# More bfloat16 filler products on TensorE: ahead of the state's update, of chunk 1's transposes, and of the rows of chunks 3, 4 and 5

## The chip, the cores and the metric

The kernel runs on one core of a Trainium2 chip. The time is device time in microseconds (us) of one execution; lower is better. The engines are named as in the profile: PE is TensorE's matrix multiplication and PEld its loading of weights, DVE is VectorE, ACT is ScalarE, POOL is GpSimd, and SP is the engine that issues the transfers between memories (SPq its queue).

## The reference

A recurrent attention layer (four sequences, eight heads, 768 steps, 40 values a head) is followed by a feed-forward layer with a leaky ReLU whose slope `alpha` differs by channel. The kernel computes the recurrence in chunks of 128 steps.

```python
for t in range(S):
    m_new = np.maximum(f[t] + m, i[t])
    f_stab = np.exp(f[t] + m - m_new); i_stab = np.exp(i[t] - m_new); m = m_new
    C = f_stab * C + i_stab * outer(v[t], k[t]);  n = f_stab * n + i_stab * k[t]
    y[t] = sigmoid(o[t]) * (C @ q[t]) / np.maximum(np.abs(n @ q[t]), 1.0)
x = y as (B * S, H * D)            # 3072 x 320
h = x @ w_in                       # 320 x 2048
g = np.maximum(h, 0) + alpha * np.minimum(h, 0)
out = g @ w_out                    # 2048 x 320
```

## The kernel before

**Tiles.** The 24 chunks (n = 0 to 23, six for each sequence) have 128 tokens and eight heads each. Two chunks make a group of 256 tokens for the feed-forward layer, twelve groups in all. For a chunk, `stage_a` brings q and k into channel order (transposes into `pq` and `pk`), `update` makes the state's increment (`pu`, from the keys `kd` weighed by their decay), and `stage_b` makes the decays `E` of the even and the odd heads (`E{n}_0`, `E{n}_1`: exponentials on ACT, the triangle cut out on POOL), the scores `pS`, their product with the decays (DVE, into `E`), the part from the state (`from_state`: `pI`, times `eT` into `T`) and the rows of the chunk (`values`: `pH`, scores times values). `T` plus `pH` gives `hv`; `gated` divides (`r`), multiplies the sigmoid of the output gate by it (`og`) and writes the rows `xn`; `x_by_channel` transposes them into `p1` and `p2`, and `split_x` cuts them into two float32r parts.

**Feed-forward.** `up` makes `ph` (2 x 256 tokens by 128 hidden channels, sixteen products), a scaled ReLU on ACT (`g`) and two DVE instructions for the leaky slope; `gh` (ACT) and `gl` (DVE for the first two groups) are its two parts. `down` adds 24 products to `po`. `fp` counts pairs of 128 hidden channels, 0 to 7. The weights are loaded as 64-bit numbers, joined on DVE from their two halves (`t_wi`, `t_wo`, `t_wr`: an ACT pass, a shift, an or) and cut into two parts (`WH`, `WL`, `OH`, `OL`, `W2`). Groups 0 and 1 run interleaved while the weights still come in.

**The gate's tile.** `og` has one buffer for a whole sequence. `load_gate(b + 1)` fills it by six transfers on SP after the last chunk of sequence b has been gated, and `open_gate` makes the sigmoid over it on ACT in one instruction, ahead of which ACT loads the table of that function.

**Buffers for products.** Attention takes its PSUM tiles from `psa`, which takes two tags in turn, with two buffers each. While group 1 of the feed-forward layer uses the buffers of tag "b", all of `psa` has the two of tag "a":

```python
turns[:] = ["a", "a"]
self.po = [ps_a.tile([P, 512], F32, tag="b", name=f"po{g}_{j}")[:, :DM] for j in range(GC)]
```

**Order.** The first group (chunks 0 and 1) is written out by hand: the words of `ORDER` name the steps, and each engine is held to that order. `warm12` in it means twelve bfloat16 products of the identity matrix (taken as 128 x 256 numbers) into a tile that nobody reads (L942). Behind that group a scheduler puts the instructions of each engine in order from its own estimate of their times, so a change at one place moves instructions far behind it; each engine then runs its instructions strictly in that order.

Of the kernel before, what the change touches and what calls it, by code (L numbers as in the profile page):

```python
# [11 lines left out]
BF16 = mybir.dt.bfloat16  # L12
# [5 lines left out]
def kernel(ctx: ExitStack, tc: tile.TileContext, q, k, v, i_gate, f_gate, o_gate, w_in, w_out, alpha, out):  # L18
    nc = tc.nc
    B, H, S, D = q.shape  # L20
    DM, DFF = w_in.shape
    P = 128
# [66 lines left out]
    def load_qk(n):  # L89
        b, c = divmod(n, NC)  # L90
        t0 = c * P
        for j, src in enumerate((q, k)):
            nc.sync.dma_start(by_token_of(n, j), src[b, :, t0 : t0 + P, :].rearrange("h p d -> p h d"))
# [30 lines left out]
    def open_gate(b, c0=0, c1=NC):  # L124
        og = o_tiles[b][:, c0:c1]
        nc.scalar.activation(og, og, AF.Sigmoid)


    def by_parity(x, par):

        return x.rearrange("p (r two) e -> p two r e", two=2)[:, par]

    kds = {}

# [14 lines left out]
    def update_steps(n):  # L149
# [22 lines left out]
        for par in range(2):  # L172
            r = slice(64 * par, 64 * par + D)
            to = by_parity(new[r], par)
            if c == 0:
                nc.vector.tensor_copy(to, by_parity(pu3[r], par))
            else:
                if n not in CP:
                    gam = gamB[r, b * H + par : (b + 1) * H : 2, c : c + 1].broadcast_to([D, NPR, VA])
                    nc.vector.tensor_tensor(to, by_parity(old[r], par), gam, ALU.mult)  # L180
                nc.vector.tensor_tensor(to, to, by_parity(pu3[r], par), ALU.add)
# [113 lines left out]
    def values(n, E, busy=lambda: None):  # L295

        pH = psa(f"pH{n}")
        va = va_t[n // GC % NV][:, n % GC]
        for i in range(H):
            if i % 2 == 0:  # L300
                busy()
            par, p = divmod(i, NPR)
            h = 2 * p + par
            nc.tensor.matmul(
                pH[:, h * VA : (h + 1) * VA], E[par][:, p * P : (p + 1) * P], va[:, h], start=True, stop=True
            )
        return pH[:, : H * VA].rearrange("p (h e) -> p h e", e=VA)
# [93 lines left out]
    def stage_b(n):  # L401
# [45 lines left out]
        if c > 0:  # L447
            *_, T = from_state(n, qf, Q)
        hv = values(n, Es) if n < NBF else values_by_parts(n, Es)
        if c > 0:  # L450
            nc.vector.tensor_tensor(T, T, hv, ALU.add)
# [61 lines left out]
    def attention(n0):  # L513
# [42 lines left out]
    SGP = range(6, 24)  # L556
    OBA = range(0)
    V0, V1 = 0, 2
    ORDER = """dq0 dq1 dw0 dw2 warm24 dv0 dw1 dw4 do1 dw3 do2 scan lf0a lf0b li0 lf0z L0 bj0 qT0 qc0 kT0 kc0 warm12 sp00
        bTt bTc l3a l3b alT l3c l3d warm6 wt0 ex00 sc00 l3e ms00 warm3 sp01 ewj ex01 ms01 sc01 warm3 eeL wg00 wTt eTt  # L560
        wTc eTc lf1a lf1b warm3 w0s wg01 sp10 alC ex10 ms10 warm3 sp11 ex11 qT1 w1s kT1 kc1 w0j0 warm4 li1 wd0 w0j1 w2s
        u0m qc1 u0c v0 w0h w0l w1j0 L1 w2j0 warm2 sc10 w1j1 warm2 w2j1 wd1 wg10 fsm fst sc11 ms11 warm6 dv1 dq3 wg11 og1
        lpa lpb bj1 dq2 dL dx2 w1h g0r dx0 g0g lpc lpd lpe g0x g0p w1l dx1 v1 x0 warm4 tadd g1r g1g s0a w2h g1x g1p w2l x1
        s1a s1d warm3 s0d og2"""

    class FeedForward:
# [196 lines left out]
    def fetch_in(i):  # L763
        if i < DFF // 512:
            pending["in", i] = [load_w_in(i, kt) for kt in range(2)] + ([] if i % 2 else [load_w_rest(i)])

    def fetch_out(fp):
        if fp < NP:
            if fp >= 2 and 2 * fp % NB == 0:
                out_block(2 * fp // NB)  # L770
            pending["out", fp] = [load_w_out(2 * fp)]
# [31 lines left out]
    def first_group():  # L803
# [125 lines left out]
        def x_first(n):  # L929
            if n == 0:  # L930
                p1.append(psa("p1_0"))
                p2.append(psa("p2_0"))
            x_by_channel(0, n, p1[0], p2[0])

        junk = ps_o.tile([P, DM], F32, tag="o0", name="warm")

        dense = ident.bitcast(mybir.dt.bfloat16)

        def warm(n=1):

            for _ in range(n):
                nc.tensor.matmul(junk[:, : 2 * P], dense[:, :P], dense, start=True, stop=True)  # L942


        t0, u0 = slice(0, GT), slice(1, GT + 1)
# [67 lines left out]
        def later_decays():  # L1013
# [26 lines left out]
            bj1=lambda: nc.gpsimd.tensor_tensor(bj[:, t1], li[:, t1], L[:, t1], ALU.subtract),  # L1040
            wt0=lambda: weights(0, GC, nc.gpsimd),
            ewj=lambda: nc.scalar.activation(wj[:, :GT], wj[:, :GT], AF.Exp),
            eeL=lambda: nc.scalar.activation(eL[:, P:GT], L[:, P:GT], AF.Exp),
            wd0=lambda: weighed(0), wd1=lambda: weighed(1),
            v0=lambda: got.update(h0=values(0, [E[0, 0], E[0, 1]], lambda: warm(V0))),
            v1=lambda: got.update(h1=values(1, [E[1, 0], E[1, 1]], lambda: warm(V1))),
            og1=lambda: open_gate(0, 0, GC), og2=lambda: open_gate(0, GC, NC),
            tadd=lambda: nc.vector.tensor_tensor(got["T"], got["T"], got["h1"], ALU.add),
            x0=lambda: x_first(0), x1=lambda: x_first(1),
# [7 lines left out]
            dq2=lambda: load_qk(2), dq3=lambda: load_qk(3), dL=lambda: nc.sync.dma_start(L_d, L),  # L1057
            dx0=lambda: fetch_out(0), dx1=lambda: fetch_out(1), dx2=lambda: fetch_in(2),
# [21 lines left out]
        for j in range(3):  # L1080
# [123 lines left out]
```

## Time and profile before

| | |
|---|---|
| median of 3 runs | 499.66 us (497.86 to 503.6) |
| the profiled execution | 500.96 us, of which 499.2 us from the first to the last instruction |
| mean granted TensorE clock | 0.990 |
| PE busy | 477.7 us (96%) |
| DVE, ACT, POOL busy | 321.6, 321.6, 304.8 us |

The busy share of PE is an average over very different stretches; what a change costs or brings is read from the stretch in which it lies. A row of the timeline has the start, the duration, the engine, the line, the operation with its operands, and in brackets how long the engine had stood idle and what ended that.

### The profile page before, as it was taken

What the parts mean: (1) busy time and instruction counts of PE and PEld (TensorE: products, weight loads), DVE (VectorE), ACT (ScalarE), POOL (GpSimd) and SP (SyncE); (2) the same over time, 40 slices, a digit from 0 to 9 for tenths busy, and PEclk for the clock granted to TensorE, in tenths of its full rate; (3) what the DMA queues carried; (4) which work ended last, traced back from release to release, by engine and by line L of the source; (5) the groups of instructions that cost most, each with busy time, mean ns of one, the idle gap of its engine ahead of it and who ended that gap; (6) DMA issues with size and microseconds to landing.
All of it is one profiled execution on the core that took longest, in us unless ns stands there. A gap on an engine that the chain in (4) does not pass through costs nothing.

```text
span 499.2 us, 11801 instructions
## 1 busy us (share of the span) xinstructions
PE 477.7 (96%) x4463; PEld 457.2 (92%) x4463; DVE 321.6 (64%) x676; ACT 321.6 (64%) x700; POOL 304.8 (61%) x393
## 2 busy tenths in 40 slices
PE   8889889989999999999899999999999999999997
PEld 7778879989989999989799999989999999999997
DVE  6889999934577686764395686567586575642321
ACT  3869697656587677756976677677886673343332
POOL 6632262306469889839498789858878755243242
PEclk9989997999999999999999999999999999999999
DMA  9999976345676566597557575769663130000000
GB/s 169 228 189 278 229 203 183 82 79 125 145 181 146 92 166 156 102 166 158 116 143 135 129 141 121 162 166 156 117 175 83 32 97 1 1 27 1 28 1 26
DMA packets 173922, 61.60 MB, mean 123 GB/s; under 512 B 140154, under 2 KB 166122, under 8 KB 173866
## 3 DMA queue, kind: packets, MB, share of 16 engines
q1 hardware_dynamic: 173786, 60.75, 55.3%
q8 instruction: 35, 0.57, 0.5%
q14 instruction: 21, 0.17, 0.1%
q10 hardware_dynamic: 80, 0.11, 0.1%
HBM read 36.90 MB, written 4.03 MB: 82 GB/s over the span
## 4 chain that ended last, share of the span: by engine, by line
PE 62%; DVE 8%; DMA 8%; ACT 8%; SPq 6%; issue 3%; POOL 3%; ACTq 0%; DVEq 0%; POOLq 0%
PE po L615 25%; PE ph L585 4%; PE ph L588 3%; PE ph L586 3%; PE ph L589 3%; PE ph L591 3%; PE ph L587 3%; PE ph L592 3%; PE ph L590 3%; DMA wo<-in_moe_w_out_dram 3%; PE pH L340 3%; PE pS L434 2%; SPq L678 2%; ACT E L418 2%; SPq L122 2%
## 5 line engine op out<-in xcount | busy, mean ns | idle before, releaser
L607 POOL TENSOR_TENSOR gl<-g,gh 128x512 fp32r<-128x512 f32 x80 | 102.9, 1287 | 62.2 <-ACT gh L606 55.0
L598 DVE SCALAR_TENSOR_TENSOR g<-g,oma,ph 128x256 f32<-128x256 f32 x160 | 69.8, 476 | 76.9 <-ACT g L594 73.1
L615 PE MATMUL po<-OH,gh 128*128 128x320 f32 x368 | 111.3, 314 | 0.0
L615 PE MATMUL po<-OL,gh 128*128 128x320 f32 x368 | 109.6, 311 | 0.0
L594 ACT ACTIVATE g<-ph 128x512 f32<-128x512 f32 x96 | 57.2, 596 | 43.7 <-PE ph L592 31.8
L615 PE MATMUL po<-OH,gl 128*128 128x320 f32 x368 | 71.9, 316 | 1.3 <-POOL gl L607 1.3
L606 ACT CAST gh<-g 128x512 fp32r<-128x512 f32 x80 | 49.5, 619 | 33.3 <-DVE g L598 32.0
L615 PEld LDWEIGHTS po<-OH,gh 128*128 128x128 f32 x368 | 69.0, 188 | 0.4 <-ACT gh L606 0.2
L615 PEld LDWEIGHTS po<-OL,gh 128*128 128x128 f32 x368 | 69.2, 188 | 0.2 <-DVE OL L714 0.2
L585 PE MATMUL ph<-XH,WH 128*128 128x256 f32 x192 | 58.5, 305 | 1.3 <-DVE g L598 0.9
L615 PEld LDWEIGHTS po<-OH,gl 128*128 128x128 f32 x368 | 56.9, 188 | 1.8 <-POOL gl L607 1.8
L418 ACT ACTIVATE E<-Lb,bT 128x128 f32<-128x128 f32 x160 | 50.9, 393 | 7.5 <-PE pH L340 7.2
L589 PE MATMUL ph<-X,W 128*128 128x256 f32 x192 | 55.2, 288 | 0.0
L586 PE MATMUL ph<-XH,WH 128*128 128x256 f32 x192 | 54.9, 286 | 0.0
L588 PE MATMUL ph<-XH,WL 128*128 128x256 f32 x192 | 54.6, 284 | 0.0
L591 PE MATMUL ph<-XL,WH 128*128 128x256 f32 x192 | 54.6, 284 | 0.0
L592 PE MATMUL ph<-X2L,W 128*128 128x256 f32 x192 | 54.5, 285 | 0.0
L587 PE MATMUL ph<-XH,WL 128*128 128x256 f32 x192 | 54.4, 284 | 0.0
L590 PE MATMUL ph<-XL,WH 128*128 128x256 f32 x192 | 54.2, 282 | 0.0
L422 POOL TENSOR_SCALAR_AFFINE_SELECT E<-E 128x512 f32<-128x512 f32 x44 | 30.0, 683 | 36.4 <-ACT E L418 36.4
L327 ACT CAST E<-pS 128x512 bf16<-128x512 f32 x72 | 41.8, 585 | 13.9 <-DVE pS L325 9.1
L585 PEld LDWEIGHTS ph<-XH,WH 128*128 128x128 f32 x192 | 36.6, 191 | 2.3 <-issue 1.1
(198 smaller groups left out, 1146.0 us busy)
## 6 DMA issues: line engine op xcount, KB each, us to landing
Lb<-L_d SPq DMA_DIRECT2D x20, 512.0 KB
wo<-in_moe_w_out_dram SPq DMA_DIRECT2D x8, 640.0 KB
wi<-in_moe_w_in_dram SPq DMA_DIRECT2D x8, 512.0 KB
qn<-in_q_dram SPq DMA_DIRECT2D x24, 160.0 KB
kn<-in_k_dram SPq DMA_DIRECT2D x24, 160.0 KB
va<-in_v_dram SPq DMA_DIRECT2D x24, 160.0 KB
og<-in_o_gate_dram SPq DMA_DIRECT2D x24, 160.0 KB
out_dram<-ob SPq DMA_DIRECT2D x11, 320.0 KB
```

The source lines that it names most:

```text
L418: nc.scalar.activation(E[:, p * P : (p + 1) * P], Lb[:, h] if Lb is not None else pb[:, p * P : (p + 1) * P], AF.Exp, bias=bT[:, c, b * H ...
L585: nc.tensor.matmul(dst, WH[half][:, 0, hs], XH[:, 0], start=True, stop=False)
L586: nc.tensor.matmul(dst, WH[half][:, 1, hs], XH[:, 1], start=False, stop=False)
L587: nc.tensor.matmul(dst, WL[half][:, 0, hs], XH[:, 0], start=False, stop=False)
L588: nc.tensor.matmul(dst, WL[half][:, 1, hs], XH[:, 1], start=False, stop=False)
L589: nc.tensor.matmul(dst, W2[:, fs], X2, start=False, stop=False)
L590: nc.tensor.matmul(dst, WH[half][:, 0, hs], XL[:, 0], start=False, stop=False)
L591: nc.tensor.matmul(dst, WH[half][:, 1, hs], XL[:, 1], start=False, stop=False)
L592: nc.tensor.matmul(dst, W2[:, fs], X2L, start=False, stop=True)
L598: nc.vector.scalar_tensor_tensor(out=y[:, e], in0=gt[:, e], scalar=oma[:, f : f + 1], in1=ph[:, e], op0=ALU.mult, op1=ALU.add)
L607: (nc.vector if g < 2 else nc.gpsimd).tensor_tensor(gl, y, gh.bitcast(F32), ALU.subtract)
L615: nc.tensor.matmul(po[j], x[:, e, j * P : (j + 1) * P], W[f // NB][:, f % NB], **ends)
```

## The change

Twelve more filler products stand in the first group ahead of `u0m` (the products of chunk 0's state update) and twelve ahead of `x1` (the transposes of chunk 1's rows). `values`, which makes the rows of chunks 2 to 5, gets filler products too: four in chunk 3, fourteen in chunk 4 and four in chunk 5, written into the very tile `pH` that the chunk's own products then overwrite.

```diff
+    def dense(dst, k):
+        x = ident.bitcast(BF16)
+        for _ in range(k):
+            nc.tensor.matmul(dst[:, : 2 * P], x[:, :P], x, start=True, stop=True)
...
     def values(n, E, busy=lambda: None):
         pH = psa(f"pH{n}")
+        dense(pH, FILL.get(n, 0))
...
+    FILL = {3: 4, 4: 14, 5: 4}
...
-        u0m qc1 u0c v0 w0h w0l w1j0 L1 w2j0 warm2 sc10 ...
+        warm12 u0m qc1 u0c v0 w0h w0l w1j0 L1 w2j0 warm2 sc10 ...
-        ... s0a w2h g1x g1p w2l x1
+        ... s0a w2h g1x g1p w2l warm12 x1
...
         def warm(n=1):
-            for _ in range(n):
-                nc.tensor.matmul(junk[:, : 2 * P], dense[:, :P], dense, start=True, stop=True)
+            dense(junk, n)
```

Behind the first group the scheduler's order changes too, on every engine, up to the middle of the first two feed-forward groups (about a fifth of the run); behind that the order is the same. Lines of the changed kernel are seven or eight higher than before (L304 is L311, for one). Three places matter for what follows.

The first is PE at the rows of chunk 4 (`pH4`). Before, the scores of the odd heads are followed at once by the rows, and these by the transposes of chunk 3's rows (`p1_1`):

```order
L438 MATMUL pS4_1_891<-qf4_709,kf0_129 128x128 x4
L304 MATMUL pH4_1002<-va0_79,E4_0_803 128x42 x4
L304 MATMUL pH4_1002<-va0_79,E4_1_885 128x42 x4
L462 MATMUL p1_1_815<-ident_72,xn1_695 128x128 x2
L358 MATMUL pI4_995<-C0_85,qf4_709 128x84 x4
```

In the changed kernel the transposes stand first, then fourteen pairs of a load and a filler product (one pair is shown), then the rows:

```order
L445 MATMUL pS4_1_919<-qf4_733,kf0_129 128x128 x4
L469 MATMUL p1_1_843<-ident_72,xn1_719 128x128 x2
L137 LDWEIGHTS ident_72
L137 MATMUL pH4_1030<-ident_72 128x256
...
L311 MATMUL pH4_1030<-va0_79,E4_0_831 128x42 x3
L469 MATMUL p2_1_844<-ident_72,xn1_719 128x128
L311 MATMUL pH4_1030<-va0_79,E4_0_831 128x42
L311 MATMUL pH4_1030<-va0_79,E4_1_913 128x42 x3
L365 MATMUL pI4_1023<-C0_85,qf4_733 128x84 x4
```

What moved: the transposes went ahead of the rows, and the fillers stand between both.

The second is DVE around the gating of chunk 5 (`r5`, then `og0`, which is the gate's tile of sequence 0). Before:

```order
L598 SCALAR_TENSOR_TENSOR ph0_5_1112<-g0_5_1129,oma_74,ph0_5_1112 128x256
L607 TENSOR_TENSOR gg1_0_1107<-ph1_0_1086,gg1_0_1107 128x512
L598 SCALAR_TENSOR_TENSOR ph0_5_1112<-g0_5_1129,oma_74,ph0_5_1112 128x256
L451 TENSOR_TENSOR T5_1465<-T5_1465,pH5_1467 128x336
L196 COPY C0_85<-pu6_1594 40x4x42 x2
L714 TENSOR_TENSOR OL3_1144<-t_wo14_1391,OH3_1143 128x640
L385 SCALAR_TENSOR_TENSOR r5_1477<-T5_1465 128x8
L389 RECIPROCAL r5_1477<-r5_1477 128x8
L607 TENSOR_TENSOR gl0_5_1134<-ph0_5_1112,gh0_5_1133 128x512
L392 TENSOR_TENSOR og0_181<-og0_181,r5_1477 128x320
```

And in the changed kernel:

```order
L615 TENSOR_TENSOR gg1_0_1149<-ph1_0_1128,gg1_0_1149 128x512
L458 TENSOR_TENSOR T5_1507<-T5_1507,pH5_1509 128x336
L722 TENSOR_TENSOR OL3_1186<-t_wo12_1367,OH3_1185 128x640
L392 SCALAR_TENSOR_TENSOR r5_1523<-T5_1507 128x8
L396 RECIPROCAL r5_1523<-r5_1523 128x8
L399 TENSOR_TENSOR og0_181<-og0_181,r5_1523 128x320
L722 TENSOR_TENSOR OL3_1186<-t_wo14_1433,OH3_1185 128x640
L606 SCALAR_TENSOR_TENSOR ph0_5_1154<-g0_5_1171,oma_74,ph0_5_1154 128x256 x2
L615 TENSOR_TENSOR gl0_5_1176<-ph0_5_1154,gh0_5_1175 128x512
L202 COPY C0_85<-pu6_1640 40x4x42 x2
```

What moved: six instructions that stood ahead of `og0` (the second `OL3`, both of `ph0_5`, `gl0_5` and the two copies of the state) now stand behind it.

The third is ACT where the gate of sequence 1 is opened (`og1`). Before, the ReLU of group 1's third pair (`g1_2`) stands ahead of it:

```order
L606 CAST gh0_6_1240<-ph0_6_1219 128x512
L594 ACTIVATE g1_2_1281<-ph1_2_1264 128x512
L126 ACT_TABLE_LOAD
L126 ACTIVATE og1_1483<-og1_1483 128x1920
L606 CAST gg1_2_1285<-ph1_2_1264 128x512
```

And in the changed kernel:

```order
L614 CAST gh0_6_1282<-ph0_6_1261 128x512
L126 ACT_TABLE_LOAD
L126 ACTIVATE og1_1529<-og1_1529 128x1920
L602 ACTIVATE g1_2_1323<-ph1_2_1306 128x512
L614 CAST gg1_2_1327<-ph1_2_1306 128x512
```

What moved: the ReLU `g1_2` went behind the table load and the sigmoid.

More of the change, by code (lines that the diff above doesn't have):

```diff
@@ L561 @@
         wTc eTc lf1a lf1b warm3 w0s wg01 sp10 alC ex10 ms10 warm3 sp11 ex11 qT1 w1s kT1 kc1 w0j0 warm4 li1 wd0 w0j1 w2s
-        u0m qc1 u0c v0 w0h w0l w1j0 L1 w2j0 warm2 sc10 w1j1 warm2 w2j1 wd1 wg10 fsm fst sc11 ms11 warm6 dv1 dq3 wg11 og1
-        lpa lpb bj1 dq2 dL dx2 w1h g0r dx0 g0g lpc lpd lpe g0x g0p w1l dx1 v1 x0 warm4 tadd g1r g1g s0a w2h g1x g1p w2l x1
+        warm12 u0m qc1 u0c v0 w0h w0l w1j0 L1 w2j0 warm2 sc10 w1j1 warm2 w2j1 wd1 wg10 fsm fst sc11 ms11 warm6 dv1 dq3 wg11 og1
+        lpa lpb bj1 dq2 dL dx2 w1h g0r dx0 g0g lpc lpd lpe g0x g0p w1l dx1 v1 x0 warm4 tadd g1r g1g s0a w2h g1x g1p w2l warm12 x1
         s1a s1d warm3 s0d og2"""
@@ L935, in first_group @@
         junk = ps_o.tile([P, DM], F32, tag="o0", name="warm")
-        dense = ident.bitcast(mybir.dt.bfloat16)
         def warm(n=1):
-            for _ in range(n):
-                nc.tensor.matmul(junk[:, : 2 * P], dense[:, :P], dense, start=True, stop=True)
+            dense(junk, n)
         t0, u0 = slice(0, GT), slice(1, GT + 1)
```

## The prediction

> **What bounds the kernel now.** The page gives PE 96% of the span, which is an average. The table by stage says more. Its columns are the stretch and its length in us, then the busy time of PE, PEld, DVE, ACT and POOL with their instructions in brackets, the granted TensorE clock, the share of the DMA engines, and GB/s.
>
> ```profile
> 27.00:57.00 30.00, 27.24 (x245) 24.56 (x245) 26.82 (x62) 21.07 (x42) 6.27 (x9) 0.94 0.99 234
> 57.00:72.00 15.00, 12.33 (x107) 10.68 (x106) 14.02 (x26) 14.92 (x39) 7.32 (x9) 1.00 0.81 205
> 72.00:98.10 26.10, 24.83 (x186) 24.55 (x187) 25.75 (x48) 19.32 (x42) 9.36 (x11) 0.87 0.54 148
> 98.10:109.90 11.80, 10.21 (x79) 9.95 (x78) 4.24 (x9) 5.96 (x8) 1.04 (x2) 1.00 0.54 100
> 109.90:499.20 389.30, 379.27 (x3648) 366.80 (x3648) 230.65 (x495) 244.72 (x537) 262.99 (x327) 1.00 0.49 106
> ```
>
> From 109.9 us on, PE is busy for 379.27 of 389.30 us at full clock, and its order there does not change. So the change is worth what it does to the moment at which that stage starts. Before it, the transfers are full to 57 us (share 0.99), ACT (14.92 of 15.00) and DVE bind to 72, DVE binds to 98.1 (25.75 of 26.10), and then nobody is full: PE waits. The chain of waits and the timelines of POOL, SP, ACT and PE show for what:
>
> ```profile
> 98.19 0.81 POOL L394 TENSOR_TENSOR xn<-T,og 128x320 f32<-128x320 f32 x1 [1.46 <-DVE og L392]
> 99.03 4.46 SPq L122 DMA_DIRECT2D og<-in_o_gate_dram  x6
> 106.30 1.28 ACT L126 ACT_TABLE_LOAD   x1 [1.53 <-DMA og<-in_o_gate_dram]
> 109.31 0.57 ACT L606 CAST gg<-ph 128x512 fp32r<-128x512 f32 x1
> 109.92 0.41 PE L615 MATMUL po<-OH,gg 128*128 128x320 f32 x1 [1.61 <-ACT gg L606]
> ```
>
> Chunk 5's rows (98.19) free the gate's only tile, its six transfers start at 99.03 and are in at 106.30, table load and sigmoid hold ACT to 109.31, and only then comes the cast for which PE idles 1.61 us. This chain starts the last stage.
>
> **The clock.** Windows cut where the granted clock changes:
>
> ```profile
> 15.55:18.96 3.41, 1.80 (x17) 1.48 (x15) 3.41 (x3) 3.40 (x11) 3.33 (x5) 1.00 0.88 192
> 18.96:22.37 3.41, 3.29 (x42) 3.26 (x43) 3.17 (x7) 3.33 (x6) 1.64 (x2) 1.00 0.93 222
> 29.20:32.61 3.41, 1.96 (x15) 1.20 (x14) 2.90 (x8) 1.94 (x5) 1.76 (x2) 1.00 1.22 274
> 32.61:36.02 3.41, 3.41 (x18) 3.41 (x17) 2.60 (x8) 3.37 (x5) 0.00 (x0) 0.50 0.33 120
> 70.16:73.57 3.41, 1.91 (x15) 1.73 (x15) 3.41 (x6) 3.33 (x8) 2.07 (x3) 1.00 0.78 149
> 73.57:76.98 3.41, 3.41 (x18) 3.41 (x18) 3.32 (x5) 3.41 (x10) 2.34 (x3) 0.50 1.06 351
> 76.98:80.39 3.41, 3.41 (x18) 3.41 (x18) 3.41 (x9) 3.29 (x8) 0.73 (x1) 0.50 0.92 237
> ```
>
> Three stretches of 3.41 us run at 0.50, which costs PE 3 x 3.41 x 0.5 = 5.1 us of work; two of them follow a stretch in which PE was busy for under 2 us. That is the most that fillers can win by the clock. The Trainium skill (TensorE: Matmul & The Clock Gate, Part 1) gives a free-running window of about 3.4 us, with which the 3.41 us here agree, and drops the clock only after an idle window, advising against gaps over some 3 us; by that, gaps under 2 us would cost nothing and these fillers would be pure extra work. The trace disagrees with the second half: 1.91 busy us of 3.41 were followed by 0.50. Yet 1.80 (15.55) was followed by full clock, so busy time alone does not settle it.
>
> **Part by part.** PE around the fillers of the first group, with the pace of a filler, and the product that waits in chunk 4 with what it waits for:
>
> ```profile
> 19.08 0.51 PE L161 MATMUL pu<-va,kd 128*40 128x42 f32 x16 [1.74 <-ACT kf L270]
> 24.46 1.04 PE L942 MATMUL warm<-ident 128*128 128x256 bf16 x8
> 25.37 0.64 PE L304 MATMUL pH<-va,E 128*128 128x42 f32 x4
> 30.62 0.41 PE L462 MATMUL p<-ident,xn 128*128 128x128 f32 x2 [1.14 <-DVE xn L394]
> 72.08 0.68 DVE L440 TENSOR_TENSOR E<-pS,E 128x512 f32<-128x512 f32 x1
> 72.81 2.98 PE L304 MATMUL pH<-va,E 128*128 128x42 f32 x16 [1.48 <-DVE E L440]
> ```
>
> A filler takes (25.37 - 24.46) / 8 = 0.114 us. **Ahead of the update**, twelve take 1.37 us, inside the 1.74 for which PE stood idle there: nothing (1.37 if that wait were gone). **Ahead of chunk 1's transposes**, 1.37 us stand against an idle time of 1.14: 0.2 us late, and the throttled stretch at 32.61 should go, 1.7 us of PE work. What is late next is not PE:
>
> ```profile
> 40.46 0.58 ACT L269 COPY kf<-pk 64x512 f32<-64x512 f32 x1 [0.98 <-PE pk L218]
> 56.48 0.79 ACT L688 ACTIVATE t_wo<-wo 128x640 f32<-128x640 f32 x1 [1.21 <-DMA wo<-in_moe_w_out_dram]
> ```
>
> ACT waited 0.98 us for PE at 40.46, the bound of this gain, and at 56.48 it waits 1.21 us for weights that come in when they come in: I take 0, between a gain of 0.98 and a loss of 0.2.
>
> **Chunk 4's fourteen**, 1.60 us, are meant for the 1.48 us of idle at 72.81. But `pH` started at the end of the DVE product at 72.08, the second half of the decays, although its first products read the first half: what it waited for is the buffer, which the odd heads' scores still held (with "a" alone, two buffers, the second tile ahead). The filler writes the same tile, so it inherits that wait and stands behind the idle time, not in it. PE then does 1.60 of filler, 1.88 of `pH` (the same 16 products at full clock, 91.20 below), and the rest: if the fillers at least spare the stretches at 73.57 and 76.98, PE gets back 3.41 and pays 1.60, which is 1.8 early at 80.5; if one stretch remains, it is where it was. What PE needs next comes from DVE, which is full there: at 87.45 it starts the products of `gh`, cast at 85.93 behind a long row of DVE work. So 0, between 1.8 gained and 1.6 lost. **Chunk 3's four**, 0.46 us, lie where PE idles 15.00 - 12.33 = 2.67 us: 0, at worst 0.46. **Chunk 5's four** wait for their buffer likewise and put 0.46 us on PE's path ahead of `pH`.
>
> **The order** moves more. DVE and PE as they were around the gating of chunk 5:
>
> ```profile
> 87.45 0.40 PE L615 MATMUL po<-OH,gh 128*128 128x320 f32 x1
> 91.20 1.88 PE L304 MATMUL pH<-va,E 128*128 128x42 f32 x16
> 97.20 0.31 PE L615 MATMUL po<-OH,gh 128*128 128x320 f32 x1
> 85.93 0.58 ACT L606 CAST gh<-ph 128x512 fp32r<-128x512 f32 x1 [0.72 <-DVE ph L598]
> 93.01 0.48 DVE L598 SCALAR_TENSOR_TENSOR ph<-g,oma,ph 128x256 f32<-128x256 f32 x1
> 93.41 0.68 DVE L607 TENSOR_TENSOR gg<-ph,gg 128x512 fp32r<-128x512 f32 x1
> 94.00 0.47 DVE L598 SCALAR_TENSOR_TENSOR ph<-g,oma,ph 128x256 f32<-128x256 f32 x1
> 94.81 0.66 DVE L196 COPY C<-pu 40x168 f32<-40x168 f32 x2
> 95.39 0.81 DVE L714 TENSOR_TENSOR OL<-t_wo,OH 128x640 fp32r<-128x640 f32 x1
> 96.12 0.62 DVE L385 SCALAR_TENSOR_TENSOR r<-T 128x8 f32<-128x8 f32 x1
> 97.02 0.69 DVE L607 TENSOR_TENSOR gl<-ph,gh 128x512 fp32r<-128x512 f32 x1
> 97.62 0.48 DVE L392 TENSOR_TENSOR og<-og,r 128x320 f32<-128x320 f32 x1
> ```
>
> Six instructions go behind `og`. By start to next start: the two `ph` 0.40 each (93.01 to 93.41), the copies 0.58, `OL` 0.73, `gl` 0.60, together **2.71 us**. DVE is full, so `og` comes 2.71 earlier, at 94.9, if its inputs keep up: `T` needs `pH`, which goes ahead of `ph0_5` on PE and so comes some 2 us earlier there. POOL's rows, the transfers and the sigmoid follow: sigmoid done at 109.31 - 2.71 = 106.60.
>
> Against this, the ReLU of the third pair now stands behind the sigmoid. Its length with what follows is read one pair earlier:
>
> ```profile
> 100.53 0.60 ACT L594 ACTIVATE g<-ph 128x512 f32<-128x512 f32 x1 [0.88 <-PE ph L592]
> 102.21 0.58 ACT L606 CAST gh<-ph 128x512 fp32r<-128x512 f32 x1 [1.08 <-DVE ph L598]
> ```
>
> From ReLU to the end of the cast: 102.79 - 100.53 = 2.26 us, where the cast alone took 0.57 (109.31): **1.65 us** are added (both ends of that price: 1.65 as read, 0 if the chain is not what PE waits for). PE goes on at 106.60 + 2.26 + 0.04 = 108.9 instead of 109.92.
>
> Would PE be there by then? Without its wait it arrived at 109.92 - 1.61 = 108.3. It has 0.46 of fillers more, and `ph0_5`, whose halves now wait behind `og`, gives its cast at 98.10 (the end of `og`) - 2.71 + 0.73 + 0.80 + 0.58 = 97.5, where PE took it at 97.20 before. So 108.3 to 108.8, just ahead of the chain: the fillers are hidden by 0.1 to 0.6 us, and if the chain came sooner they would cost up to 0.46.
>
> **Sum:** -2.71 + 1.65 = -1.06 us. The profiled execution took 500.96, so 499.9 on its terms; it stands 1.30 above the median of the three runs shown, so I forecast 499.66 - 1.06, about **498.6 us**.
>
> **Rivals.** (a) *PE's work binds after all* and the clock comes back. For: PE too is busy for 24.83 of 26.10 us there. Against: 25.75 busy us of 26.10 on DVE. 5.1 won, 1.60 + 0.46 + 0.46 paid, the order's 1.06 on top: 499.66 - 3.6 = 496.0, with all fillers hidden 493.5. (b) *The sigmoid blocks ACT and the gate is not earlier*: one wait takes the place of another. ACT's queue is strict, so a late `og` transfer holds `g1_2` too: +1.65, 501.3. It turns slower once chunk 5's gating gains less than 1.65 us, for which it is enough that `pH`, behind fillers which wait for their buffer, comes late to `T`. For: the order on ACT is certain, the 2.71 rest on DVE staying full. Against: DVE's idle is 0.35 us in 26. (c) *The fillers don't hold the clock* where it matters: they stand behind the wait in chunk 4, so the half-idle stretch remains, and one or two stretches stay at 0.50. PE then has no slack, up to 1.6 lost against 1.06 won: 499.7. The Trainium skill (the same page and section) lets the window start anywhere from run to run, by which a filler put in one place would help in some runs only; the three times, 497.86 to 503.6, would fit, but no trace here shows two phases.
>
> **Chances.** Forecast 0.50, (a) 0.15, (b) 0.17, (c) 0.18. The range goes from (a) without its best end to (b) with the runs' scatter: 495.0 to 502.0. A change within 1% is what a measurement of this kernel can hardly tell from none: under 494.7 only the better end of (a), with scatter, 0.10; over 504.7 only (b) with a bad draw, 0.04; between, 0.86.
>
> **What would show it.** In the changed profile: the fillers of chunk 4 start at the end of the second `E` product, with the idle time still ahead of them; the stretch behind chunk 1's transposes at full clock; the first transfer of the gate near 96.3 instead of 99.03; table load and sigmoid, then a ReLU, two DVE halves and a cast, and PE waiting for that cast to about 108.9. It would be wrong if PE went on before 107.5 (then the clock counts) or after 110.5 (then the gate was not earlier), or if the stage behind it took other than about 389 us.

## The result, and the profile after

The changed kernel takes **497.17 us** (median of 19 executions, 495.93 to 502.23), the kernel before on the same chip 501.3: a ratio of **0.9928** (95% interval 0.9906 to 0.9951), about 3.6 us less. Two later comparisons on other occasions gave 0.9911 (0.988 to 0.9943) and 0.9923 (0.989 to 0.9955). The time forecast was 498.6. The profiled execution of the changed kernel took 498.75 us, with a span of 497.0 and a mean granted clock of 0.997 (0.990 before).

The table by stage, in the same columns as the one of before (busy time of PE, PEld, DVE, ACT and POOL, the clock, the DMA share, GB/s), with the last stage as its last row:

```profile
57.00:72.00 15.00, 12.93 (x117) 11.79 (x117) 12.72 (x28) 13.92 (x36) 5.77 (x8) 1.00 0.83 221
72.00:98.10 26.10, 23.86 (x185) 22.27 (x184) 25.49 (x45) 19.76 (x43) 11.69 (x13) 0.93 0.53 150
98.10:109.90 11.80, 11.80 (x98) 11.56 (x97) 5.27 (x11) 6.37 (x8) 0.70 (x2) 1.00 0.62 113
109.90:497.00 387.10, 379.12 (x3655) 367.24 (x3653) 231.67 (x497) 245.41 (x539) 263.19 (x327) 1.00 0.48 106
```

Only one stretch of 3.41 us at 0.50 is left, inside 72.00 to 98.10 (0.93; before it was 0.87, and another stretch stood at 32.61). The fillers and the chain of the gate, from the timelines of PE, SP and ACT:

```profile
73.53 0.44 PE L469 MATMUL p<-ident,xn 128*128 128x128 f32 x2 [1.11 <-POOL xn L401]
74.47 2.69 PE L137 MATMUL pH<-ident 128*128 128x256 bf16 x14 [0.51 <-DVE E L447]
98.59 4.83 SPq L122 DMA_DIRECT2D og<-in_o_gate_dram  x6
106.38 1.28 ACT L126 ACT_TABLE_LOAD   x1 [1.14 <-DMA og<-in_o_gate_dram]
109.39 0.58 ACT L602 ACTIVATE g<-ph 128x512 f32<-128x512 f32 x1
111.04 0.58 ACT L614 CAST gg<-ph 128x512 fp32r<-128x512 f32 x1 [1.08 <-DVE ph L606]
111.68 0.41 PE L623 MATMUL po<-OH,gg 128*128 128x320 f32 x1 [0.93 <-ACT gg L614]
```

PE goes on at 111.68, which is 1.76 us **later** than before (109.92), and still the kernel ends 2.2 us earlier: the rest took 385.3 us instead of 389.3. So in this pair of profiles the gain lies wholly in the stage that the forecast held constant. What that means, and whether it holds for other executions, is what the experiments are about. The change forecast was 1.06 us, the measured one 3.6; the two times lie close because the forecast started from three executions with a median of 499.66 us, and the nineteen have one of 501.3.

### The profile page after: what moved, and what is told of

The parts are those of the page before. It is cut to its first block, busy times and chain, and to the rows that moved or that the text cites. A ratio compares the mean times of both kernels' runs of the same rounds, so it can differ in the third digit from the quotient of the medians.

```text
span 497.0 us, 11890 instructions
## 1 busy us (share of the span) xinstructions
PE 479.6 (97%) x4509; PEld 458.3 (92%) x4509; DVE 324.1 (65%) x676; ACT 321.4 (65%) x700; POOL 305.9 (62%) x393
## 4 chain that ended last, share of the span: by engine, by line
PE 64%; DVE 10%; ACT 8%; POOL 6%; DMA 5%; issue 5%; SPq 1%; ACTq 0%; DVEq 0%; POOLq 0%
PE po L623 25%; PE ph L593 4%; PE ph L596 3%; PE ph L594 3%; PE ph L597 3%; PE ph L599 3%; PE ph L595 3%; PE ph L600 3%; PE ph L598 3%; PE pH L347 2%; PE pS L441 2%; POOL gl L615 2%; PE warm L137 2%; DMA kS<-Z 2%; DMA qS<-Z 1%
## 5 line engine op out<-in xcount | busy, mean ns | idle before, releaser
L596 PE MATMUL ph<-XH,WL 128*128 128x256 f32 x192 | 54.1, 282 | 0.0
L599 PE MATMUL ph<-XL,WH 128*128 128x256 f32 x192 | 53.9, 281 | 0.0
L595 PE MATMUL ph<-XH,WL 128*128 128x256 f32 x192 | 53.7, 280 | 0.0
L598 PE MATMUL ph<-XL,WH 128*128 128x256 f32 x192 | 53.5, 279 | 0.0
```

Source lines behind the costliest of these rows:

```text
L595: nc.tensor.matmul(dst, WL[half][:, 0, hs], XH[:, 0], start=False, stop=False)
L596: nc.tensor.matmul(dst, WL[half][:, 1, hs], XH[:, 1], start=False, stop=False)
L598: nc.tensor.matmul(dst, WH[half][:, 0, hs], XL[:, 0], start=False, stop=False)
L599: nc.tensor.matmul(dst, WH[half][:, 1, hs], XL[:, 1], start=False, stop=False)
```

## The experiments

In all kernels that are neither the one before nor the changed one, every engine is held to a written order (dependencies without a wait, added at the end of the program), so that an edit does not move the scheduler's choices. The measured ratios are against the kernel before on the same chip; "clock" is the median over the executions of one kernel.

| kernel | new fillers | ratio (95% interval) | median us | clock |
|---|---|---|---|---|
| before, again | 0 | 0.9982 (0.9947 to 1.0017) | 500.99 | 0.985 |
| order alone | 0 | 1.0015 (0.9978 to 1.0052) | 501.90 | 0.984 |
| fillers alone, old order | 46 | 0.9957 (0.9923 to 0.9992) | 500.57 | 0.989 |
| changed, again | 46 | 0.9911 (0.988 to 0.9943) | 498.48 | 0.996 |
| twelve ahead of the update | 12 | 0.9965 (0.9936 to 0.9994) | 500.55 | 0.986 |
| both twelves | 24 | 0.9973 (0.9941 to 1.0006) | 501.25 | 0.990 |
| changed, ReLU first | 46 | 0.9887 (0.9844 to 0.993) | 497.27 | 0.998 |
| changed, fourteen moved | 46 | 0.9957 (0.9919 to 0.9995) | 501.03 | 0.990 |
| two gaps filled | 66 | 1.0017 (0.9979 to 1.0054) | 502.98 | 0.996 |
| two gaps filled, ReLU first | 66 | 1.0015 (0.9981 to 1.0049) | 502.42 | 0.997 |
| changed, third time | 46 | 0.9923 (0.989 to 0.9955) | 498.27 | 0.997 |
| two gaps, long fillers | 46 | 0.9905 (0.987 to 0.994) | 498.67 | 0.998 |

From the profile of each come the stretches at half clock ahead of the last stage, the gate's first transfer, and two numbers counted from the end of PE's order, which is the same in all kernels there: when its 3640th product from the end starts, and how long it takes from there to the last one. Where a stretch at 0.50 lies inside that time, its lost half is taken off (marked *), as if PE bound there throughout.

| profile | at 0.50: start (length), us | gate | 3640th | to the last |
|---|---|---|---|---|
| before | 32.6 (3.4), 73.6 (6.8) | 99.03 | 111.2 | 384.3 |
| before, again | 20.5 (10.2), 37.6 (3.4), 78.5 (6.8) | 103.67 | 115.8 | 383.6 |
| order alone | 21.3 (10.2), 65.7 (6.8), 82.8 (3.4) | 103.65 | 118.5 | 382.3 |
| fillers alone | 40.8 (3.4), 74.9 (10.2) | 103.42 | 118.1 | 382.0* |
| twelve | 32.0 (3.4), 73.0 (10.2) | 97.30 | 111.5 | 383.2* |
| both twelves | 75.5 (6.8) | 96.55 | 110.8 | 382.9* |
| changed | 75.0 (3.4) | 98.59 | 113.0 | 380.3 |
| changed, again | 73.8 (3.4) | 97.76 | 112.1 | 380.7* |
| changed, third | none | 96.74 | 111.0 | 380.9 |
| ReLU first | 75.4 (3.4) | 98.89 | 112.7 | 381.3 |
| fourteen moved | 85.8 (13.7) | 98.89 | 116.3 | 381.2 |
| gaps, 66 fillers | none | 96.10 | 110.3 | 385.8 |
| the same, ReLU first | 61.9 (6.8) | 100.20 | 114.1 | 383.9* |
| gaps, long | 76.1 (3.4) | 97.30 | 111.8 | 381.7 |

### The kernel before, again

No edit; the question is how far executions of one kernel differ, and where.

> The kernel before once more, for a second profile and for the granted clock of every run. In the two profiles so far the last stage, whose order is the same, is 4.0 us shorter after the change (PE restarts at 111.7 against 109.9, yet the span ends 2.2 us earlier). Theory C (clock): the time of a run follows the clock it lost, one to one: runs at a mean clock of 0.990 are about 5 us slower than runs at 1.000, ratio 1.00 in all. Theory O (order): the clock of a run says nothing on its time. Theory L (later stage by chance): the waits behind 110 us (8.0 us in all in the first profile) come out differently in this profile of the very same kernel, by 2 us or more.

Its profiled execution took 504.84 us. Windows around the update, and then the timeline of PE at the update and at chunk 1's transposes:

```profile
17.10:20.51 3.41, 1.67 (x28) 1.34 (x26) 3.41 (x2) 3.35 (x10) 3.41 (x5) 1.00 1.08 249
20.51:23.92 3.41, 3.41 (x18) 3.35 (x18) 3.17 (x7) 3.21 (x5) 0.77 (x1) 0.50 1.03 179
...
27.34:30.75 3.41, 3.41 (x18) 2.97 (x18) 1.52 (x5) 0.00 (x0) 0.43 (x1) 0.50 1.35 204
```

```profile
19.77 0.51 PE L161 MATMUL pu<-va,kd 128*40 128x42 f32 x16 [1.74 <-ACT kf L270]
20.20 3.38 PE L304 MATMUL pH<-va,E 128*128 128x42 f32 x16
35.42 0.41 PE L462 MATMUL p<-ident,xn 128*128 128x128 f32 x2 [1.40 <-DVE xn L394]
```

The same program, the same wait of 1.74 us ahead of the update, but here three windows at 0.50 follow it (20.51 to 30.75), and chunk 1's transposes start at 35.42 instead of 30.62: **4.8 us late**, which the gate's first transfer keeps (103.67 against 99.03). The execution from which the forecast was made did not have this stretch. The windows begin at other places: 32.61 there and 37.58 here, which is 1.6 us apart in a step of 3.41. So the same 1.74 us of idle time cost nothing in one execution and 5 us in another; what is seen to differ is where the windows start. From the 3640th product on the two profiles are within 0.7 us of each other (384.3 and 383.6), so Theory L, by which the late stage of one kernel varies by 2 us or more, did not come true in this pair.

### The order alone, and the fillers alone

```diff
 (order alone: the kernel before, no new filler)
+    for engine, text in FORCED.items():        # the changed kernel's order
+        ... tc.add_manual_dep(i, before_it.name, NoSync)
 (fillers alone: the changed kernel's 46 fillers)
+    for engine, text in FORCED.items():        # the order of the kernel before
```

> No filler is added; every engine is held to the order of the changed kernel. Theory O: the gain is in the order, so 0.993, and the first transfer of the gate of sequence 1 comes 0.5 to 2.7 us earlier than in the kernel before. Theory C: the clock falls as before (mean 0.988 to 0.994), ratio 0.997 to 1.003. If both work, 0.995 to 0.997.

> All 46 fillers at their places, every engine held to the order of the kernel before. Theory O: nothing to gain, 1.000 to 1.002. Theory C: mean clock 0.996 or more and 0.993. The prediction's sum gave the fillers nothing (0 to +0.5 us).

The order alone shows no gain (1.0015; from 0.9978, so one of the forecast 1.06 us isn't excluded), at the clock of the kernel before (0.984). Its profile has the stretch behind the update too, as much time at 0.50 as the kernel before run again (20.5 us), and the gate's first transfer at the same time (103.65, 103.67). That does not tell what the order does to the gate, since the half clock lies elsewhere: only in the profile of the order alone does a stretch stand at 65.7, behind which DVE waits 1.35 us (at 70.05) and 2.04 us (at 73.20). Profiles without the stretch behind the update tell it, further down. The fillers alone gain part (0.9957, between the two theories): the stretch behind the update is gone, but the clock fell for 10.2 us in chunk 4, where the old order leaves PE's idle time in one piece (1.49 us; in the new order it comes as 1.11 and 0.51 with work between). Here the stretch was dear: DVE waited 1.74 us at 80.40 and 1.50 us at 82.33, and the gate came at 103.42.

### The changed kernel, again

> The changed kernel once more: 0.993 as measured. Theory C: mean clock 0.996 to 1.000, and its slower runs are those with the lower clock. Theory L: the waits behind 110 us (4.5 us in its first profile) differ by 2 us or more in this profile.

0.9911, beside 0.9928 in the first comparison; Theory L did not come true here either (380.3 and 380.7 us to the last product). Up to here one reading fitted: within one kernel the time follows the clock that it lost (one less the mean clock, times the span), by 0.6 to 0.9 us for each us, and lines through the executions of each kernel met near 496 to 497 us at full clock. For the kernel before that is far outside its data: none of its 122 executions with a listed clock got above 0.993, and only one above 0.990.

### Which fillers

```diff
-    FILL = {3: 4, 4: 14, 5: 4}
+    FILL = {}
-        ... s0a w2h g1x g1p w2l warm12 x1      (left in where both twelves stay)
+        ... s0a w2h g1x g1p w2l x1
```

> The order of the changed kernel on every engine, but of its 46 new fillers only the twelve ahead of chunk 0's update; those ahead of chunk 1's transposes and those of chunks 3, 4 and 5 are gone. Order alone gave 1.0015 of the kernel before, with 8.7 us of clock lost (one less the mean granted clock, times the span); all fillers gave 0.9911 with 2.1 us lost. Theory C (the clock): in the profiles of the kernel before run again and of order alone, PE ran 10.2 us at 0.50 from 20 us on, behind a wait of 1.74 us for which it stood idle ahead of the update, which is 5.1 us lost; with all fillers that stretch ran at full clock. These twelve should keep it so: some 4 us lost, 0.7 us of time for each us won back, so about 3 us faster than before, 0.994. Theory U (all groups are needed, since the clock falls at the next gap if not at this one): lost 7 to 9, ratio 0.998 to 1.002. Theory L (what differs is waits in the late stage that vary by execution): no relation to the lost clock, ratio anywhere between 0.991 and 1.001.

> The order of the changed kernel, with both twelves of the first group, without the fillers of chunks 3, 4 and 5. Theory C: the stretches behind the update and behind chunk 1's transposes at full clock, the one of chunk 4 (from about 74 us, 3.4 to 10 us at 0.50 in the profiles so far) stays: 2 to 3.5 us lost, ratio 0.992 to 0.994. By the step of the prediction that put chunk 4's fillers behind the idle time, where they don't fill it, the loss there should be as with them, so that the ratio comes to that of the whole change, 0.991 to 0.992. If these fillers hold the clock in chunk 4, this kernel loses 1.5 to 3 us more clock than the whole change and is 0.2 to 0.4% above it.

The twelve ahead of the update gain 0.35% (0.06 to 0.64) by themselves; the twelve ahead of the transposes add nothing that can be told (0.9973). The profile of the one has a stretch at 32.0, behind the transposes, that of the other none there, and the gate differs by 0.75 us. The long stretches in chunk 4 (10.2 and 6.8 us) hardly held the gate back: 97.30 and 96.55, where the profile without any stretch has 96.74. The rest of the gain, some 0.5%, appears only with the fillers of chunks 3 to 5. That contradicts the clock as the only cause: they shorten one stretch that, in these two profiles, costs little. Both ratios came out above what the expectations by the clock had (0.994, and 0.992 to 0.994).

### One ReLU back ahead of the sigmoid

ACT's order: `g1_2` ahead of the table load, as before the change.

```diff
-ACT: ... gh0_6, ACT_TABLE_LOAD, og1, g1_2, gg1_2 ...
+ACT: ... gh0_6, g1_2, ACT_TABLE_LOAD, og1, gg1_2 ...
```

> The changed kernel with one instruction moved: ACT's ReLU of group 1's third pair (g1_2) ahead of the table load and the sigmoid, as before the change. In its two profiles PE went on at 111.68 and 110.79 us, behind waits of 0.93 and 0.51 us for the cast that follows this ReLU. Theory S (the sigmoid's block costs what PE waits there): the cast comes 1.65 us earlier, PE arrives at 110.3 to 110.7 without a wait, 0.5 to 0.9 us are won: 0.990 of the kernel before where the whole change had 0.991, and the profile shows no wait of PE for that cast or one under 0.3. Theory W (PE's work from there on is paced by its other waits): the next product or a later one waits instead, same time as the changed kernel.

```profile
107.14 0.60 ACT L602 ACTIVATE g<-ph 128x512 f32<-128x512 f32 x1 [1.37 <-PE ph L600]
107.76 1.28 ACT L126 ACT_TABLE_LOAD   x1
110.77 0.56 ACT L614 CAST gg<-ph 128x512 fp32r<-128x512 f32 x1
```

The ReLU's products come only at 107.14, so now the ReLU holds the table load, and the cast is 0.27 us earlier (110.77 against 111.04), not 1.65. The ratio, 0.9887 from six executions, can't be told from the changed kernel's. Neither theory's size was right: a wait changed its place.

Together the profiles give the price of each step of this chain. The kernel before has DVE's `og` of chunk 5 at 97.62, POOL's rows at 98.19 (0.81 us), the first transfer at 99.03, the table load at 106.30 and the 3640th product at 111.21. The third profile of the changed kernel, without any stretch at 0.50, has that product at 110.99 and, from the timelines of DVE, POOL, SP and ACT:

```profile
94.81 0.49 DVE L399 TENSOR_TENSOR og<-og,r 128x320 f32<-128x320 f32 x1
95.39 1.33 POOL L401 TENSOR_TENSOR xn<-T,og 128x320 f32<-128x320 f32 x1 [0.87 <-DVE og L399]
96.74 4.37 SPq L122 DMA_DIRECT2D og<-in_o_gate_dram  x6
104.40 1.28 ACT L126 ACT_TABLE_LOAD   x1 [0.60 <-DMA og<-in_o_gate_dram]
```

So `og` is 2.81 us earlier; from it to the gate it takes 1.93 us instead of 1.41 (0.5 more), from the gate to the table load 7.66 instead of 7.27 (0.4 more), and from the table load to the 3640th product 6.59 instead of 4.91 (1.7 more). That makes -0.2 us, as the two products say (110.99 and 111.21). The last of these steps is the ReLU's: it takes 6.58 to 6.59 us in all nine profiles with the sigmoid first, and 4.90 to 4.91 with the ReLU first (both of the kernel before, and both with the ReLU moved back; the profile of the fillers alone has a stretch at 0.50 in it). With the ReLU moved back the table load comes 8.87 us behind the gate, so that little of this 1.7 is won.

### The fourteen moved into the gap

```diff
-    FILL = {3: 4, 4: 14, 5: 4}
+    FILL = {3: 4, 5: 4}
             pS = psa(f"pS{n}_{par}")
+            dense(pS, 14 if (n, par) == (4, 1) else 0)
```

> The changed kernel with chunk 4's fourteen fillers moved: ahead of the odd heads' scores (into that tile, pS4_1) instead of ahead of the rows (pH4). There PE has what follows to do at once, so the scores come 1.6 us later and the idle times of 1.11 and 0.51 us behind them shrink. Theory G (the gap counts: the clock falls when PE idles too much in a window of 3.41 us): no stretch at 0.50 between 70 and 90 us, lost clock under 1 us where the changed kernel had 1.4 to 2.1, PE early at 80 us by up to 1.6, time 0.3 to 1 us under the changed kernel, 0.989 to 0.990 of the kernel before. Theory D (DVE is full there and takes the late scores late): the product of scores and decays starts at 74.0 to 75.3 instead of 73.74 and everything of DVE behind it is late by up to 1.6 us: 0.991 to 0.994.

```profile
70.65 1.69 PE L137 MATMUL pS<-ident 128*128 128x256 bf16 x14
74.08 0.86 PE L311 MATMUL pH<-va,E 128*128 128x42 f32 x6 [0.63 <-DVE E L448]
86.75 0.63 PE L624 MATMUL po<-OH,gh 128*128 128x320 f32 x1 [2.82 <-ACT gh L615]
```

There is no stretch at 0.50 in chunk 4 any more, and DVE is 1.27 us ahead (its first `ph` product at 83.64 instead of 84.91). But PE, earlier still, now waits 2.82 us at 86.75, and behind **that** gap the clock fell for 13.7 us, which made DVE wait 1.83 us for chunk 5's rows and gave all of it back. Its executions fall into groups: four of twelve took 496.8 to 498.0 us at a clock of 0.997, seven 500.7 to 503.2 at 0.986 to 0.990, and one 500.4 at 1.000.

### Both gaps filled, and the time that did not come

```diff
             pS = psa(f"pS{n}_{par}")
+            dense(pS, {(4, 1): 14, (5, 1): 20}.get((n, par), 0))
```

> The changed kernel with chunk 4's fourteen fillers ahead of the odd heads' scores of chunk 4 (pS4_1), as in the run before, and twenty more (2.3 us) ahead of those of chunk 5 (pS5_1). In the run with the fourteen moved alone, no stretch between 70 and 85 us ran at 0.50 and DVE was 1.27 us ahead of the changed kernel (its first ph product at 83.64 instead of 84.91), but PE then stood idle for 2.82 us at 86.75 and ran 13.6 us at 0.50 from there. Theory G (the gap counts, wherever it is): the twenty leave 0.5 us of that idle time, the stretch from 86 us runs at full clock, DVE keeps its 1.3 us to the gate, whose first transfer comes at about 97.3 instead of 98.59, and PE goes on at about 110.4 instead of 111.68; lost clock under 1 us; 0.988 to 0.990 of the kernel before, 0.5 to 1.3 us under the changed kernel. Theory M (the idle time moves on once more): the clock falls at the next place where PE is early, 2 to 4 us lost, 0.991 to 0.996.

> The same with the ReLU of group 1's third pair (g1_2) ahead of the table load and the sigmoid. In the run with the ReLU moved alone, it held back the table load (107.76 us, right behind the ReLU's end) and the cast came at 110.77 instead of 111.04, with no wait of PE for it left over 0.3 us. If DVE and the gate are 1.3 us earlier here, the gate's data come at 105 while the ReLU can't start before its products (107.14 in that run), so that the ReLU holds the sigmoid by 1 to 2 us and the cast comes no earlier than with the sigmoid first: Theory S (ReLU first is worth what PE waited) 0.3 to 0.9 us under the run without it; Theory H (it holds the gate) 0 to 1 us above it.

> The changed kernel once more, so that the two others are compared with it on the same chip: 0.991 of the kernel before (0.988 to 0.994), lost clock 1 to 2.5 us. Theory F (the windows of the clock start anywhere): its runs fall into groups, those at a clock of 0.999 to 1.000 at 496 to 497.5 us, and those with one stretch at 0.50 or more 1 to 3 us above.

Of the third set of the changed kernel, the five executions at a clock of 0.999 to 1.000 took 496.5 to 498.3 us and the other seven 498.1 to 500.6, close to the groups of Theory F. With both gaps filled, the first half came as expected: full clock through chunks 4 and 5, the gate at 96.10, PE in its last stage at 110.3.

```profile
72.00:98.10 26.10, 24.85 (x211) 23.50 (x211) 25.12 (x47) 19.10 (x42) 10.66 (x14) 1.00 0.55 156
109.20:499.80 390.60, 378.41 (x3648) 366.44 (x3647) 230.74 (x495) 244.49 (x537) 263.09 (x327) 1.00 0.49 105
```

And yet 502.98 us at a clock of 0.996 (502.42 with the ReLU first as well, which can't be told from it: there the ReLU held the table load to 109.20, 8.99 us behind the gate). With no more clock to lose, it is 4.7 us slower than the changed kernel beside it: **the reading by the clock alone fell here**. The last stage has the same order, the same work (378.41 us of PE) and full clock, and is 4.9 us longer than that of the changed kernel's third profile, of which these are the row of that stage and, from the timelines of SP and ACT, what ACT waits for at 175 us:

```profile
109.90:495.60 385.70, 378.32 (x3648) 366.46 (x3647) 230.69 (x495) 244.69 (x537) 263.60 (x327) 1.00 0.49 107
```

```profile
171.10 1.26 SPq L244 DMA_TRANSPOSE kS<-Z  x1
174.69 0.46 ACT L236 CAST Z<-qn 128x320 bf16<-128x320 f32 x1 [2.72 <-DMA kS<-Z]
```

The timelines of the kernel with 66 fillers: PE's wait at 149 us with what it goes back to, and then the same place as above:

```profile
136.47 1.27 SPq L244 DMA_TRANSPOSE kS<-Z  x1
140.85 0.20 POOL L230 MEMSET Z<- 128x128 bf16 x1 [1.19 <-DMA kS<-Z]
149.01 0.21 PE L347 MATMUL pH<-vb,E 128*128 128x126 bf16 x1 [0.95 <-POOL vb L325]
172.02 1.28 SPq L244 DMA_TRANSPOSE kS<-Z  x1
177.11 0.46 ACT L236 CAST Z<-qn 128x320 bf16<-128x320 f32 x1 [4.34 <-DMA kS<-Z]
179.62 0.87 DVE L607 SCALAR_TENSOR_TENSOR g<-g,oma,ph 128x256 f32<-128x256 f32 x2 [2.30 <-ACT g L603]
180.64 0.36 PE L594 MATMUL ph<-XH,WH 128*128 128x256 f32 x1 [1.55 <-DVE r L395]
```

From the transposing transfer of `kS` to the cast that waits for it: 177.11 - 172.02 = 5.1 us here, 174.69 - 171.10 = 3.6 there. Four places (PE at 149, 181, 271 and 334 us) make up 4.1 of the 4.9 us. Three of them stand at the same products in the other kernel with 66 fillers; the kernels with no, 12 or 24 fillers lose at places of their own, and those with 46 at few. The kernels with 66 and with 46 fillers run the same order from there on; what differs by then is how many instructions PE has behind it. It gets them in packets of 16384 bytes on a queue of their own (packets, MB, share of the DMA engines):

```profile
q8 instruction: 36, 0.59, 0.5%
```

(35 packets in the kernel before and in the changed one.) Twenty fillers are 40 more instructions, so each packet comes some 20 products earlier in the order: in the trace one starts at 174.88 us, between the transfer and the cast above, and one at 137.80, beside the earlier transfer of `kS`, which lands 4.25 us after its issue (3.28 in the other kernel), keeps POOL idle for 1.19 us (0.19 there) and so makes POOL late for PE at 149. The Trainium skill (Trainium Architecture — The Big Picture, The software stack) gives 64 bytes for an instruction. By that a packet holds 16384 / 64 = 256; the trace of the changed kernel agrees, with 9143 recorded instructions of PE and 35 packets (9143 / 256 = 35.7). The packets come all through the run.

### The same gaps with fewer, longer fillers

```diff
+    def dense_long(dst, k):
+        x = ident.bitcast(BF16)
+        wide = x[:, None, :].broadcast_to([P, 2, 2 * P])
+        for _ in range(k):
+            nc.tensor.matmul(dst, x[:, :P], wide, start=True, stop=True)
...
             pS = psa(f"pS{n}_{par}")
+            dense_long(pS, {(4, 1): 7, (5, 1): 7}.get((n, par), 0))
```

> As the run with both gaps filled, but with seven fillers of 512 columns ahead of the odd heads' scores of chunk 4 and seven ahead of those of chunk 5, in place of fourteen and twenty of 256: the two gaps get 1.6 us each, and PE has 46 new fillers in all, as in the changed kernel, instead of 66. The run with 66 reached the last stage 1.4 us ahead of the changed kernel at full clock and still took 503.0 us, since its last stage was longer. Counted from PE's 3640th product from its end to its last, where the order of all engines is the same in all kernels, the profiles give 384.3, 383.6 and 382.3 us without new fillers, 383.2 and 382.9 with 12 and 24 (less the 1.7 us of a stretch at 0.50), 380.3 to 381.3 in six profiles with 46, 385.8 and 383.9 with 66. The losses come at the same products for kernels with the same number of fillers, next to a packet of 16384 bytes of PE's instructions on the queue of kind instruction. Theory I (the number of instructions ahead shifts the loading of instructions against the transfers that PE and ACT wait for): with 46 the last stage is 380.3 to 381.5 again, PE passes that product at 110 to 111 us, and the time is 495 to 497.5, 0.986 to 0.991 of the kernel before. Theory P (it is the place of the fillers, the scores' tiles or PE's being early): the last stage stays at 383.9 to 385.8, and the time at 500 to 503, 0.998 to 1.002.

```profile
70.29 1.67 PE L143 MATMUL pS<-ident 128*128 128x512 bf16 x7
84.06 1.68 PE L143 MATMUL pS<-ident 128*128 128x512 bf16 x7
```

```profile
110.70:497.20 386.50, 378.42 (x3648) 366.47 (x3647) 230.56 (x495) 244.41 (x537) 263.06 (x327) 1.00 0.49 106
```

Fillers at the same two places, but 46 in number: the last stage is back at 381.7 us, the ratio at 0.9905, where 66 had 1.0017. So it was not the place of the fillers but their **number** that made the last stage long. (One number in the expectation was off: of the stretch in the profile of the fillers alone only 1.1 us lie behind the 3640th product, so its value is 382.0. And the time, 498.67 us, lies above the 495 to 497.5 expected, the product at 111.8 instead of 110 to 111.) Nor was it PE's being early: the profiles with 46 pass the 3640th product anywhere between 111.0 and 118.1 us, those with 66 at 110.3 and 114.1.

That a packet of instructions delays a transfer which runs beside it is borne out by the fourteen traces. Their last stage has 36 transposing transfers of `kS` and `qS`, 504 in all. The 118 with a packet that starts within 3.0 us of their issue landed 4.04 us after it (median), the other 386 after 3.27; for 27 of the 36 there are profiles of both kinds, and with the packet the transfer took longer in 25, by 0.83 us in the mean. With 66 fillers twelve transfers meet a packet in this way, in the other profiles six to nine. No run moved a packet by itself, so this is read from a comparison, and not from an edit.

As a version that beats both kernels it fails: it can't be told from the changed kernel (0.9905 and 0.9923, with intervals that overlap), and one stretch at 0.50 came back at 76.1.

## Why the prediction was right or wrong

The time came within the range, 1.4 us under the point forecast, but that is luck: the sum's -1.06 us was not there (the start of the last stage moved by -0.2 at full clock), and the 3.6 to 4.5 us that were gained came from two places to which the sum gave nothing. Step by step:

- **"From 109.9 us on ... its order there does not change. So the change is worth what it does to the moment at which that stage starts."** The step that failed most. The same order took 382.3 to 384.3 us from the 3640th product on in three profiles without new fillers, and 380.3 to 382.0 in seven with 46: means of 383.4 and 381.2, so about 2.2 of the 3.6 to 4.5 us gained lie there. That the number of PE's instructions sets this is shown between 66 and 46; between 0 and 46 it rests on these profiles.
- **Ahead of the update: "nothing", since the fillers lie inside an idle time.** Failed, and it is the other part of the gain. The idle time itself was the cost: in two of three profiles without the twelve the clock fell behind it for 10.2 us, in the one with the same order 4.8 us late at chunk 1's transposes; in all eleven with them it did not. The sum priced the stretches that one execution had, and that execution lacked the dearest.
- **"by that, gaps under 2 us would cost nothing" (the Trainium skill, TensorE: Matmul & The Clock Gate, Part 1) against "The trace disagrees".** The trace's side held. Windows with 1.67 to 1.93 us of PE work were followed by 0.50, others with 1.80 or 1.95 were not. The other half of that page's rule, a window that starts anywhere, which the forecast could see no trace for, is what the profiles show.
- **Ahead of chunk 1's transposes: the stretch should go, worth 0.** Right on both: full clock from 30.75 to 41 us in every profile of the changed kernel, and nothing gained by adding them (0.9965 to 0.9973).
- **Chunk 4's fillers stand behind the idle time and are worth 0.** The place was right: 74.47, at the end of the second `E` product, with 1.11 and 0.51 us of idle time ahead. In the new order DVE did hide the stretches there (the gate at 97.30 and 96.55 with 10.2 and 6.8 us at 0.50, at 96.74 with none); in the old order, with the fourteen behind the wait, it did not (DVE idle for 1.74 and 1.50 us, the gate at 103.42).
- **`og` 2.71 us earlier by the order.** Right in size: 94.61 to 95.36 in the profiles of the twelve, of both twelves and the third of the changed kernel, against 97.62 and a forecast of 94.9. In the first of the changed kernel, with a stretch at 75.0, it came at 96.66. What failed is that "POOL's rows, the transfers and the sigmoid follow" at their old lengths: the rows and the transfers took 0.5 and 0.4 us more.
- **The ReLU behind the sigmoid costs 1.65.** Right: 1.68 from the table load to the 3640th product (the sum's own rows give 2.26 - 0.57 = 1.69). With the 0.9 us above, it uses up what `og` had gained.
- **Rivals.** (a), the clock coming back, was nearest, in its sign and its time (496.0), but by a stretch that the profile did not show; it had 0.15. Of (b) it is true that the start of the last stage gained nothing (PE at 111.68 in the profile, past the bound of 110.5 beyond which the forecast called itself wrong), and that did not decide the time. (c) was wrong in the main: the fillers hold the clock (median 0.996 to 0.999 against 0.980 to 0.985), though a stretch in chunk 4 stayed in two of three profiles of the changed kernel, as it said. Its 499.7 is not what its terms give: 499.66 + 1.6 - 1.06 = 500.2.

Open: how often the stretch behind the update comes in the kernel before. Of its 122 executions with a listed clock 71 were below 0.985, with a median of 503.9 us, and 51 at or above it, with 500.5; the profiles with the stretch had 0.978 and 0.980, the one without had 0.990, so it may be more than half. The better group is still 2.4 us over the changed kernel's three sets (498.06), which fits the 2.2 us of the last stage and not the lines that met at full clock. What a stretch of 10.2 us costs is read from one profile for each place, and the split of the gain in two parts is one of means, good to about 1 us.

## What to carry to other kernels

A profile is one execution: before a gap is priced at nothing because that execution ran through it at full clock, profile the kernel twice or compare the clock of many executions. Fill idle time where TensorE is what the rest waits for, and look for the next gap that being early opens. When an order brings one step of a chain forward, price every step behind it anew: here a step 2.8 us earlier left 0.2. An edit that only adds instructions can change a stage far behind it, of the same order and work; before such a gain is credited to its purpose, try the same edit with another number of instructions.

## What the runs showed of the hardware

- The granted clock changes in windows of 3.413 us, whose start differs from execution to execution (32.61 and 37.58 us in two of the same kernel). In the fourteen profiles, of the windows at full clock (without the first and the last of a run) 33 had PE busy for 1.5 to 2.1 us: 17 of them were followed by 0.50 and 16 by full clock, so busy time alone does not settle it. All three with less than 1.5 were followed by 0.50, four of 114 with 2.1 to 2.9, and none of 1825 with more. The clock then stayed at 0.50 for one to four windows, even where PE was busy throughout.
- The fall of the clock went with the gap: filling the one at 72 us moved it from 75 to 86 us, and made it 13.7 us long instead of 3.4.
- PE's instructions arrive while it runs, in packets of 16384 bytes about every 13 us; a transposing transfer beside which one started took 0.83 us longer than the same transfer without, in the mean of 27; 40 instructions more ahead of a stage of 381 us made it 2.7 to 4.6 us longer, with the same order and the same work, and with the one stretch at half clock taken off.
